# A planned two-layer long-convolution and MLP kernel: reserved engines for the first chunk, a shorter first normalisation, two half blocks that may alternate, and plain fp32 inverse transforms

## The chip, the cores and the metric

The kernel runs on one core of a Trainium2 chip. The metric is the device time of one execution in microseconds, the median of several runs. The profile shown is of one further execution, recorded by the hardware profiler.

## The reference, cut to what matters

The input is a sequence of 2048 positions with 640 channels. Two kinds of layer alternate, each twice, each with a normalisation ahead of it and a residual sum behind it:

```python
def _A_ref(q, k, v, shift_k, ssm_k, ssm_D):
    # k_shift: causal depthwise conv of k with 4 taps
    kv = k_shift * v
    # y: causal depthwise conv of kv with a kernel as long as the sequence, by FFT
    y = y + kv * ssm_D[None, None, :]
    return q * y
def _B_ref(x, w1, w2):
    h = jnp.einsum("bsd,df->bsf", x, w1)          # 640 -> 1728
    h = jnp.maximum(h, 0)
    return jnp.einsum("bsf,fd->bsd", h, w2)       # 1728 -> 640

x = A_q
x = x + _A_ref(_layernorm(x), A_k, A_v, A_shift_k, A_ssm_k, A_ssm_D)
x = x + _B_ref(_layernorm(x), B_w1, B_w2)
x = x + _A_ref(_layernorm(x), A_k, A_v, A_shift_k, A_ssm_k, A_ssm_D)
x = x + _B_ref(_layernorm(x), B_w1, B_w2)
```

The long convolution `y` doesn't depend on `x`, so both layers of kind A use the same one. All of it is in float32.

## The kernel before

**Tiling.** The sequence is cut into 8 chunks of 256 positions, each of two halves of 128 rows, and the channels into 5 tiles of 128 (`NDT`). A convolution unit is a chunk with one or two channel tiles, or two chunks with one tile. There are 21 units; `rank(u)` is a unit's place in their list, and the first three are chunk 0, the next three chunk 1.

**The convolution.** `transform(u)` loads `kt`, `vt` and the filter `hf`, adds the term `dD` to one row of `hf`, forms the taps (`acc`, `tp`), and takes a forward transform of the signal and of the filter by matmuls with constant matrices (`pg`, `pt`, `pr`). The results `at` and `gt` are spilled to memory as `A` and `G`. `products(u)` multiplies the transforms of all earlier chunks in pairs and adds them (`Ax`, `Gx`, `pd`, `pacc`, all on VectorE), forms `u`, and takes the inverse transform by matmuls into `pq`; `qs`, `ys` and `Y` are its results. Two forms of the inverse transform are there. A unit with `rank(u) < FU` is transformed in plain fp32: `cM` times `u`, which the trace shows as two records a matmul. A unit of a higher rank has `u` split in two parts of fewer bits, `uh` on ScalarE and `ul` on VectorE, and three matmuls (`mm3`) for each of the plain one's. `FU` is 10, so 11 of the 21 units take the split form, with two such groups each.

**The MLP.** The weights are loaded as fp32 (`ws`, 28 tiles of 128x640), their norm is taken by matmuls (`pw`, `pn`), and from it a scale. Each is then split in two fp16 parts (`wsplit`): the high part `w[:, 0]` on ScalarE, the low part `w[:, 1]` on VectorE. Activations are split in the same way (`xh` after the normalisation, `hh` and `hl` after the first matmul), and each product takes three matmuls. `main(n, ...)` is one MLP block. The first eight (n = 0 to 7: chunk 0 and 1, both layers, both halves apart) have 128 rows, the other twelve 256. A block goes through 7 pieces of the hidden dimension in the order `JS`: `mm1` fills `h` from the transposed input `xT`, ScalarE and VectorE make `hh` and `hl`, and `mm2` adds into `o` and `oc`. Block n starts with its first matmul into `h`.

**Chunk 0 and the head.** Nothing of the MLP can start before chunk 0's convolution is done for the first half. Its result is multiplied by the normalised input (`xnA`) and added to `x`, with the row sums in `sp`; then come the second normalisation (`sums`, `negmB`, the square `jkB`, `stdB`, the reciprocal and a Newton step on VectorE: `newton` with `fast`, then `xnB`), the split `xh`, two groups of five transposes on TensorE, and their copies to `xT`.

**What sets the order.** Every operation is given to `Plan` with an engine, an estimated cost and a priority class (`URGENT` 0, `SOON` 1, `BACK` 1.7, `SPILL`, `CONV`, `LATER`, `FILL`). `Plan.order` runs through an estimated time and, whenever an engine is free, takes from the candidates that are ready the one of the best class; the instructions are then written out in that order, and each engine runs its own in order. Buffers are rings (`Ring`): a ring's tiles are taken in the order of the program, within a `stream`; tiles of different streams may overtake each other.

Of the kernel before, what the change touches and what calls it, by code (L numbers as in the profile page):

```python
# [11 lines left out]
F32 = mybir.dt.float32  # L12
# [31 lines left out]
MODE = 0  # L44
POOLMOD = 5
STT = ((0, 0), (0, 2), (0, 4))
FA = 6
FU = 10
# [29 lines left out]
class Op:  # L78
    __slots__ = ("eng", "cost", "fn", "prio", "seq", "deps", "outs", "new", "tiles", "left", "ready", "start", "nbytes")


class Plan:
# [5 lines left out]
    def op(self, eng, cost, fn, reads=(), writes=(), prio=0, nbytes=0):  # L88
        o = Op()
        o.eng, o.cost, o.fn, o.seq, o.nbytes = eng, cost, fn, len(self.ops), nbytes  # L90
        o.prio = (prio, o.seq)
        deps, o.new, o.outs = set(), [], []
        for t in reads:
            if t.writer is not None:
                deps.add(t.writer)
        for t in writes:
            if t.writer is not None:
                deps.add(t.writer)
            elif t.ring is not None and not t.left:
# [10 lines left out]
        o.left, o.ready = len(deps), 0.0  # L110
        for d in deps:
            d.outs.append(o)
        self.ops.append(o)

    def order(self):
        engs = sorted({o.eng for o in self.ops})
        free = dict.fromkeys(engs, 0.0)
        cand = {e: [] for e in engs}
        for o in self.ops:
            if not o.left:  # L120
                cand[o.eng].append(o)
# [3 lines left out]
        while n < len(self.ops):  # L125
# [18 lines left out]
            for e in engs:  # L144
# [20 lines left out]
                if best.nbytes:  # L165
                    dma = max(dma, now + 1.9) + best.nbytes / 360e3
                    end = dma + 1.1
                if e == "PE":
# [22 lines left out]
def tile_h3_mlp(ctx: ExitStack, tc: tile.TileContext, q, kT, vT, shk, hF, hR, dD, w1, w2, cM, cG, out):  # L191
# [117 lines left out]
    def transform(u):  # L309
# [33 lines left out]
        for i, (c, t) in enumerate(u):  # L343
            if c == 0:
                dve(P, lambda i=i, t=t: DVE.tensor_add(hf[0:1, i, 0:P], hf[0:1, i, 0:P], dDs[:, t, :]), [dDs, hf], [hf], pr_)
# [32 lines left out]
        if c0:  # L378
            for b in range(2):

                def f(b=b):
                    for ri in range(2):
                        for eo in range(2):
                            m = cXt[:, ri, :] if b and eo else cGt[:, 2 * eo + ri, :]
                            PE.matmul(e4(pg[b])[:, :, ri, :], m, hv(hf)[:, eo], start=ri + eo == 0, stop=ri + eo == 2)  # L385

                pe(16 * mm4, f, [hf, cGt, cXt], [pg[b]], pr_)
                act(w, lambda b=b: ACT.activation(gt[:, :, 0:2, b, :], e4(pg[b]), AF.Copy), [pg[b]], [gt], pr_)
# [78 lines left out]
    def products(u, at, gt, after):  # L467
        n, nm = len(u), "%d_%d" % u[0]
        pr_ = (URGENT, CONV, LATER)[min(u[0][0], 2)]
        w, h = 2 * n * P, n * P  # L470
        mm, mm4 = (0.109, 0.109) if n == 2 else (0.213, 0.0545)
# [42 lines left out]
        pq = T(ps, "tr", 2, [P, 512], "pq" + nm, stream=1)  # L514
        for ri in range(2):
# [30 lines left out]
        qs = T(cv, "qs", 1, [P, n, P], "qs" + nm)  # L546
        act(h, lambda: ACT.activation(qs.t, pq[:, 256 : 256 + h].rearrange("p (a b) -> p a b", a=n), AF.Copy), [pq], [qs], pr_)
        direct = u[-1][0] == 0
        if direct:
# [5 lines left out]
            yo = lambda s: dst[s][:, t0 * P : t0 * P + h].rearrange("p (a b) -> p a b", a=n)  # L555
        else:
            ys = T(cv, "u", 2, [P, 2, n, P], "ys" + nm)
            dst = [ys, ys]
            yo = lambda s: ys[:, s]
        pp = lambda: pq[:, 0:h].rearrange("p (a b) -> p a b", a=n)  # L560
        dve(h, lambda: DVE.tensor_sub(yo(0), pp(), qs.t), [pq, qs], [dst[0]], pr_)
        dve(h, lambda: DVE.tensor_add(yo(1), pp(), qs.t), [pq, qs], [dst[1]], pr_)
# [10 lines left out]
        if direct:  # L573
            xs, xns, sp0 = first[c]
            cs = slice(t0 * P, t0 * P + h)
            for s in range(2):
                dve(h, lambda s=s: DVE.tensor_mul(xns[s][:, cs], xns[s][:, cs], dst[s][:, cs]), [xns[s], dst[s]], [xns[s]], (URGENT, BACK)[s])
                dve(h, lambda s=s: DVE.scalar_tensor_tensor(xs[s][:, cs], xns[s][:, cs], 1.0, xs[s][:, cs], op0=ALU.mult, op1=ALU.add, accum_out=sp0[s][:, 0, t0 // 2 : t0 // 2 + 1]), [xns[s], xs[s]], [xs[s], sp0[s]], (URGENT, BACK)[s], 0.2)
# [52 lines left out]
    def wsplit(k):  # L631
        for j in JS:
            for i in range(2):
# [3 lines left out]
                s = lambda: sc[k].t.bitcast(F32)  # L637
# [16 lines left out]
    def stats(xs, sums, name, S, pr=0, fast=False):  # L654
# [8 lines left out]
        if fast:  # L663

            def newton():
                stt = DVE.scalar_tensor_tensor
                r_, v_ = r[:, q_], v[:, q_]
                DVE.reciprocal(r_, sd[:, q_])
                stt(v_, ssq[:, q_], D * EPS, r_, op0=ALU.add, op1=ALU.mult)
                stt(v_, v_, -0.5 / D, r_, op0=ALU.mult, op1=ALU.mult)  # L670
                stt(r_, v_, 1.5, r_, op0=ALU.add, op1=ALU.mult)
                DVE.tensor_mul(nmr[:, q_], negm[:, q_], r_)

            dve(0, newton, [sd, ssq, negm], [r, v, nmr], pr, 0.9)
        else:
            dve(0, lambda: DVE.reciprocal(sd[:, q_], sd[:, q_]), [sd], [sd], pr, 0.15)

            def newton():
                ACT.activation(v[:, q_], ssq[:, q_], AF.Identity, scale=-0.5 / D, bias=heps.t)
                cols = [slice(s, s + 1) for s in S]  # L680
                for c in cols:
                    ACT.activation(r[:, c], v[:, c], AF.Identity, scale=sd[:, c])
                for c in cols:
                    ACT.activation(v[:, c], r[:, c], AF.Identity, scale=sd[:, c], bias=c15.t)
                for c in cols:
                    ACT.activation(r[:, c], v[:, c], AF.Identity, scale=sd[:, c])
                for c in cols:
                    ACT.activation(nmr[:, c], r[:, c], AF.Identity, scale=negm[:, c])

            act(0, newton, [ssq, sd, negm, heps, c15], [v, r, nmr], pr, 0.15 + 0.8 * len(S))  # L690
# [18 lines left out]
    SUMS = {}  # L709

    def prep(a, layer, S, pr=0):
# [20 lines left out]
        xns = stats(xs, sums2, "B" + nm, S, pr, head)  # L732
        hl = {}
        for s in S:
# [10 lines left out]
        if not head or S[0]:  # L745
            for x in range(2):
                for s in S:
                    dma(1280, lambda s=s, x=x: SP.dma_start(xt[x][:, :, (s - S[0]) * P : (s - S[0]) * P + P], hl[s][:, x, :], transpose=True), [hl[s]], [xt[x]], pr)
            return xT, S
        for x in range(2):  # L750
            pt = T(ps, *(("x", 1), ("o0", 1))[x], [P, NDT, P], f"xt{nm}{x}", F16, stream=1)

            def f(x=x, pt=pt):
                for t in range(NDT):
                    PE.transpose(pt[:, t, :], hl[0][:, x, t * P : t * P + P], ident16.t)

            pe(0.29, f, [hl[0], ident16], [pt], pr)
# [6 lines left out]
    def main(n, a, layer, S, xTS):  # L764
# [7 lines left out]
        oc = T(ps, "oc", 1, [P, 2, P], f"oc{n}")  # L772
# [20 lines left out]
        def mm1(j, i, p):  # L793
            tail = j == NFP - 1 and i == 1
            z = slice(i * R, i * R + R)

# [12 lines left out]
        for j in JS:  # L809
            p = T(ps, "h", 2, [P, 2 * R], f"h{n}_{j}")  # L810
            hh = T(mlp, "hh", NH, [P, 2 * R], f"hh{n}_{j}", F16)
            hl = T(mlp, "hl", NH, [P, 2 * R], f"hl{n}_{j}", F16)
# [22 lines left out]
        xs = X[a]  # L835
        nm = f"{a}_{layer}_{S[0]}"
        sp = T(mlp, "sp", 2, [P, 2, 2], f"sp{nm}") if layer == 0 else None
        for s in S:
            for h in range(2):

                def f(s=s, h=h):
                    d = ds[h]
                    acc = {"accum_out": sp[:, s, h : h + 1]} if layer == 0 else {}
                    DVE.scalar_tensor_tensor(xs[s][:, d], o(s, h), inv.t, xs[s][:, d], op0=ALU.mult, op1=ALU.add, **acc)

                dve(128 if h else 512, f, [oc if h else ob[s], inv, xs[s]], [xs[s]] + ([sp] if layer == 0 else []), URGENT, 0.15)
# [41 lines left out]
    def early(a):  # L888
        sums = load_x(a)
        first[a] = (X[a], stats(X[a], sums, f"A{a}_0", both, URGENT, True), [keep(const, [P, 1, 3], f"sp{a}_{s}") for s in range(2)])  # L890
# [10 lines left out]
    if MODE == 1:  # L901
        xTs.append(prep(0, 0, (1,), BACK))
# [102 lines left out]
```

## Time and profile before

| | |
|---|---|
| median of 3 runs | 875.25 us (875.15 to 875.81) |
| profiled execution | 875.43 us |
| its span in the trace | 873.7 us |
| TensorE busy | 852.4 us, 98% |
| VectorE busy | 707.5 us, 81% |
| ScalarE busy | 434.3 us, 50% |
| GpSimd busy | 1.8 us |

In the trace PE is TensorE's matmuls, PEld its weight loads, DVE VectorE, ACT ScalarE, POOL GpSimd, SP the queue that issues the DMAs; L801 is line 801 of the kernel. A row of a timeline has the start in us, the duration in us, engine, line, operation, what it writes and reads, the shape, the count, and in brackets the idle time of the engine before it with what ended it. Matmuls overlap: their rate is read from start to start, not from their durations.

### The profile page before, as it was taken

How to read it: one execution, taken by the hardware profiler on the slowest of the kernel's cores; microseconds unless marked ns; L12 is line 12 of the kernel's file. 1: busy time of each engine (PE TensorE's matmuls, PEld its weight loads, DVE VectorE, ACT ScalarE, POOL GpSimd, SP SyncE). 2: the span in 40 equal slices, each digit the busy share in tenths (PEclk: the TensorE clock that was granted, in tenths of full speed). 3: DMA queues.
4: the chain of work that ended last, by engine and by line, in shares of the span. 5: the costliest groups of instructions: out<-in, count | busy, mean ns of one | idle time of the engine just before them, and what ended most of it. 6: DMA issues, size and time to landing. Idle time of an engine off the chain costs nothing.

```text
span 873.7 us, 19067 instructions
## 1 busy us (share of the span) xinstructions
PE 852.4 (98%) x7676; PEld 652.6 (75%) x7676; DVE 707.5 (81%) x1262; ACT 434.3 (50%) x1031; POOL 1.8 (0%) x14
## 2 busy tenths in 40 slices
PE   8689999999999999999999999999999999999997
PEld 7678787787777777777777777777777777777775
DVE  7999999999989999999999999999888833323111
ACT  6497587446466364636446281825325245425010
POOL 0000000000000000000000000000000000000000
PEclk9989999999999999999999999999999999999999
DMA  9966858987997664853655947383888821201000
GB/s 324 395 240 209 275 176 287 271 298 255 302 277 221 219 208 155 248 176 133 163 192 172 235 128 199 106 247 103 254 275 258 251 73 32 61 2 31 32 1 31
DMA packets 122219, 164.12 MB, mean 188 GB/s; under 512 B 49681, under 2 KB 78609, under 8 KB 122130
## 3 DMA queue, kind: packets, MB, share of 16 engines
q1 hardware_dynamic: 122130, 162.90, 60.1%
q8 instruction: 60, 0.98, 0.5%
q14 instruction: 29, 0.24, 0.1%
HBM read 117.05 MB, written 35.65 MB: 175 GB/s over the span
## 4 chain that ended last, share of the span: by engine, by line
PE 70%; DVE 14%; DMA 8%; ACT 4%; issue 2%; SPq 1%; DVEq 0%; ACTq 0%
PE h L801 10%; PE h L802 10%; PE h L804 10%; PE o L786 8%; PE o L787 8%; PE o L789 7%; DMA Gx<-G 4%; DVE pd L510 3%; PE oc L786 2%; PE oc L787 2%; DVE pacc L511 2%; PE oc L789 2%; PE pq L531 2%; PE pg L407 2%; PE pg L385 1%
## 5 line engine op out<-in xcount | busy, mean ns | idle before, releaser
L801 PE MATMUL h<-xT,w 128*128 128x256 f16 (+1 forms) x1400 | 322.9, 252 | 0.5 <-ACT xT L761 0.5
L802 PE MATMUL h<-xT,w 128*128 128x256 f16 (+1 forms) x1400 | 322.6, 252 | 0.5 <-DMA xT<-xh 0.5
L804 PE MATMUL h<-xT,w 128*128 128x256 f16 (+1 forms) x1300 | 303.8, 252 | 0.0
L786 PE MATMUL o<-w,hh 128*128 128x512 f16 x448 | 170.0, 380 | 0.0
L787 PE MATMUL o<-w,hh 128*128 128x512 f16 x448 | 169.8, 379 | 0.0
L816 ACT ACTIVATE hh<-h 128x512 f16<-128x512 f32 (+1 forms) x120 | 60.6, 505 | 211.4 <-PE h L804 210.9
L789 PE MATMUL o<-w,hl 128*128 128x512 f16 x416 | 157.8, 379 | 1.9 <-DVE hl L817 1.9
L802 PEld LDWEIGHTS <-w 128*128 128x128 f16 x1400 | 137.4, 98 | 10.6 <-issue 0.6
L801 PEld LDWEIGHTS <-w 128*128 128x128 f16 x1400 | 137.3, 98 | 10.1 <-DMA xT<-xh 0.2
L804 PEld LDWEIGHTS <-w 128*128 128x128 f16 x1300 | 127.5, 98 | 9.7 <-issue 0.9
L817 DVE SCALAR_TENSOR_TENSOR hl<-h,hh 128x512 f16<-128x512 f32 (+1 forms) x120 | 69.4, 579 | 79.2 <-ACT hh L816 78.1
L511 DVE TENSOR_TENSOR pacc<-pacc,pd 128x768 f32<-128x768 f32 x140 | 132.9, 950 | 0.7
L787 PEld LDWEIGHTS <-hh 128*128 128x128 f16 x896 | 87.7, 98 | 56.2
L786 PEld LDWEIGHTS <-hh 128*128 128x128 f16 x896 | 87.6, 98 | 55.1 <-issue 0.7
L789 PEld LDWEIGHTS <-hl 128*128 128x128 f16 x832 | 81.4, 98 | 52.4 <-DVE hl L817 3.2
L787 PE MATMUL oc<-w,hh 128*128 128x128 f16 x448 | 98.2, 219 | 0.0
L786 PE MATMUL oc<-w,hh 128*128 128x128 f16 x448 | 98.1, 219 | 0.0
L789 PE MATMUL oc<-w,hl 128*128 128x128 f16 x416 | 91.1, 219 | 0.0
L510 DVE TENSOR_TENSOR pd<-Ax,Gx 128x768 f32<-128x768 f32 x87 | 81.5, 950 | 7.0 <-DMA Gx<-G 6.9
L339 ACT ACTIVATE tp<-kt,shs 128x256 f32<-128x256 f32 (+1 forms) x78 | 43.7, 574 | 13.8 <-DVE acc L368 6.2
L510 DVE TENSOR_TENSOR pd<-at,Gx 128x768 f32<-128x768 f32 x44 | 41.3, 949 | 0.1
L660 ACT ACTIVATE jkA<-x,negmA 128x640 f32<-128x640 f32 x32 | 26.3, 822 | 20.9 <-DVE negmA L657 20.7
(159 smaller groups left out, 1171.1 us busy)
## 6 DMA issues: line engine op xcount, KB each, us to landing
Ax<-A SPq DMA_DIRECT2D x91, 384.0 KB, 4.0
Gx<-G SPq DMA_DIRECT2D x91, 384.0 KB, 4.2
G<-gt SPq DMA_DIRECT2D x32, 384.0 KB, 3.4
A<-at SPq DMA_DIRECT2D x32, 384.0 KB, 4.3
y<-Y SPq DMA_DIRECT2D x30, 320.0 KB, 3.5
ws<-in_w SPq DMA_DIRECT2D x28, 320.0 KB, 6.7
x<-in_q SPq DMA_DIRECT2D x16, 320.0 KB, 3.9
out_dram<-x SPq DMA_DIRECT2D x16, 320.0 KB, 3.0
```

Source lines behind the costliest of these rows:

```text
L339: ACT.activation(o[:, i : i + m], kview(i, m, j), AF.Copy, scale=shs[:, t, j : j + 1])
L510: ew(f"mac{j % POOLMOD}", 768, lambda e, pd=pd, av=av, gv=gv: e.tensor_mul(pd.t, av(), gv()), [ax, gx], [pd], pr_)
L511: dve(768, lambda i=i, pd=pd: DVE.tensor_add(acc[:, i], acc[:, i], pd.t), [acc, pd], [acc], pr_)
L660: act(D, lambda s=s, jk=jk: ACT.activation(jk.t, xs[s].t, AF.Square, bias=negm[:, s : s + 1], accum_out=ssq[:, s : s + 1]), [xs[s], negm], ...
L786: PE.matmul(z, hh[:, c], wh[:, d], start=(j == JS[0] and i == 0 and (h == 0 or s == S[0])), stop=False)
L787: PE.matmul(z, hh[:, c], wl[:, d], start=False, stop=end and tail)
L789: PE.matmul(z, hl[:, c], wh[:, d], start=False, stop=end)
L801: PE.matmul(p[:, z], wh, xv(t, 0), start=b, stop=False)
L802: PE.matmul(p[:, z], wh, xv(t, 1), start=False, stop=tail and e)
L804: PE.matmul(p[:, z], wl, xv(t, 0), start=False, stop=e)
L816: act(2 * R, lambda p=p, hh=hh: ACT.activation(hh.t, p.t, AF.Relu), [p], [hh], URGENT)
L817: dve(2 * R, lambda p=p, hh=hh, hl=hl: DVE.scalar_tensor_tensor(hl.t, p.t, 0.0, hh.t, op0=ALU.max, op1=ALU.subtract), [p, hh], [hl], URGENT)
```

## The change

It has four parts.

1. **Reserved engines.** A new class `CRIT` of -1 is given to chunk 0's `transform` and `products` and to the first half's `prep`. While an operation of that class is about to become ready on an engine (all that it depends on has started), the planner doesn't start one of a lower class there whose estimated cost is more than the remaining time plus `SLACK`. The addition of `dD` to `hf` goes from VectorE (5 operations) to GpSimd (3 operations). The second half's `yd` goes to class `BACK`. `wsplit` is called once, behind the first half's `prep`, and splits the pieces of the two weights alternately, the second two pieces (`WLAG`) behind the first. The estimated costs of matmuls (`mm`, `mm4`) are raised.
2. **A shorter first normalisation.** For chunk 0's first layer, `prep` writes no normalised `xnB`. VectorE subtracts the mean (`xc`) beside ScalarE's square; `xh` and the low part `xl` come from `xc` times the reciprocal of the root. The Newton step is left to a factor for each row (`FAC`) that is applied when the block's result is added to `x`. The normalisation `xnA` of chunk 0 loses its Newton step on VectorE (`fast`) and has the ScalarE one of the other chunks.
3. **The first two half blocks may alternate.** Block 1 has streams of its own for `h`, `hh`, `hl` and `oc`. Block 0's first piece is issued as two operations, high part of `xT` first.
4. **Inverse transforms.** `FU` is 99: all 21 units are transformed back in plain fp32.

```diff
-MODE = 0
+WLAG = 2
+CRIT, SLACK = -1, 0.6
-FU = 10
+FU = 99
@@ Plan.order
+        soon = {e: [o for o in self.ops if o.eng == e and o.prio[0] == CRIT] for e in engs if e != "SP"}
...
+                rooms = [(max(d.ready for d in o.deps) - now + SLACK, o.prio) for o in soon.get(e, ()) if o.left and all(d.start is not None for d in o.deps)]
                 for o in cand[e]:
                     if best is not None and o.prio > best.prio:
+                        continue
+                    if any(o.cost > room and o.prio > prio for room, prio in rooms):
                         continue
@@ transform, products
-        pr_ = (URGENT, CONV, LATER)[min(u[0][0], 2)]
+        pr_ = (CRIT, CONV, LATER)[min(u[0][0], 2)]
-        mm, mm4 = (0.109, 0.109) if n == 2 else (0.213, 0.0545)
+        mm, mm4 = (0.128, 0.113) if n == 2 else (0.213, 0.063)
-        for i, (c, t) in enumerate(u):
-            if c == 0:
-                dve(P, lambda i=i, t=t: DVE.tensor_add(hf[0:1, i, 0:P], hf[0:1, i, 0:P], dDs[:, t, :]), [dDs, hf], [hf], pr_)
+        if c0:
+            t0 = u[0][1]
+            gps(h, lambda: POOL.tensor_add(hf[0:1, :, 0:P], hf[0:1, :, 0:P], dDs[:, t0 : t0 + n, :]), [dDs, hf], [hf], pr_)
@@ wsplit
-    def wsplit(k):
-        for j in JS:
+    def wsplit():
+        ks = [(JS[x - y * WLAG], y) for x in range(NFP + WLAG) for y in range(2) if 0 <= x - y * WLAG < NFP]
+        for j, k in ks:
@@ prep, chunk 0's first layer
+            dve(D, lambda: DVE.tensor_scalar(xc.t, xs[s].t, negm[:, 0:1], None, op0=ALU.add), [xs[s], negm], [xc], pr)
+            act(1, lambda: ACT.activation(sd[:, 0:1], ssq[:, 0:1], AF.Sqrt, scale=1.0 / D, bias=epst.t), [ssq, epst], [sd], pr, 0.1)
+            dve(1, lambda: DVE.reciprocal(r[:, 0:1], sd[:, 0:1]), [sd], [r], pr, 0.15)
+            act(D, lambda: ACT.activation(w.t, xc.t, AF.Copy, scale=r[:, 0:1]), [xc, r], [w], pr)
+            dve(D, lambda: DVE.scalar_tensor_tensor(v.t, xc.t, r[:, 0:1], w.t, op0=ALU.mult, op1=ALU.subtract), [xc, r, w], [v], pr, 0.13)
...
+            dve(0, factor, [ssq, r, inv], [fac, FAC[a, s]], CONV, 0.6)
@@ main
-        oc = T(ps, "oc", 1, [P, 2, P], f"oc{n}")
+        sm = 3 if n == 1 else 0
+        oc = T(ps, *(("x", 1) if n == 1 else ("oc", 1)), [P, 2, P], f"oc{n}", stream=sm)
...
-            p = T(ps, "h", 2, [P, 2 * R], f"h{n}_{j}")
+            p = T(ps, "h", 2, [P, 2 * R], f"h{n}_{j}", stream=sm)
@@ the order of the program
-    wsplit(0)
-    xTs = [prep(0, 0, (0,))]
-    if MODE == 0:
-        xTs.append(prep(0, 0, (1,), BACK))
-    wsplit(1)
+    xTs = [prep(0, 0, (0,), CRIT)]
+    xTs.append(prep(0, 0, (1,), BACK))
+    wsplit()
```

More of the change, by code (lines that the diff above doesn't have):

```diff
@@ L78 @@
 class Op:
-    __slots__ = ("eng", "cost", "fn", "prio", "seq", "deps", "outs", "new", "tiles", "left", "ready", "start", "nbytes")
+    __slots__ = ("eng", "cost", "fn", "prio", "seq", "deps", "outs", "new", "tiles", "left", "ready", "start", "nbytes", "deps")
 class Plan:
@@ L109, in op @@
         deps.discard(o)
-        o.left, o.ready = len(deps), 0.0
+        o.left, o.ready, o.start, o.deps = len(deps), 0.0, None, deps
         for d in deps:
@@ L167, in order @@
                     end = dma + 1.1
+                best.ready = end
+                if best.prio[0] == CRIT and e in soon:
+                    soon[e].remove(best)
                 if e == "PE":
@@ L379, in transform, with f @@
             for b in range(2):
-                def f(b=b):
-                    for ri in range(2):
+                for ri in range(2):
+                    def f(b=b, ri=ri):
                         for eo in range(2):
@@ L652, in small, with stats @@
         return T(mlp, tag, 2, [P, 2], name)
-    def stats(xs, sums, name, S, pr=0, fast=False):
+    def stats(xs, sums, name, S, pr=0):
         q_ = slice(S[0], S[-1] + 1)
@@ L661, in stats, with newton @@
         act(2, lambda: ACT.activation(sd[:, q_], ssq[:, q_], AF.Sqrt, scale=1.0 / D, bias=epst.t), [ssq, epst], [sd], pr, 0.1)
[L663 to L690, printed above, removed]
+        dve(0, lambda: DVE.reciprocal(sd[:, q_], sd[:, q_]), [sd], [sd], pr, 0.15)
+        def newton():
+            ACT.activation(v[:, q_], ssq[:, q_], AF.Identity, scale=-0.5 / D, bias=heps.t)
+            cols = [slice(s, s + 1) for s in S]
+            for c in cols:
+                ACT.activation(r[:, c], v[:, c], AF.Identity, scale=sd[:, c])
+            for c in cols:
+                ACT.activation(v[:, c], r[:, c], AF.Identity, scale=sd[:, c], bias=c15.t)
+            for c in cols:
+                ACT.activation(r[:, c], v[:, c], AF.Identity, scale=sd[:, c])
+            for c in cols:
+                ACT.activation(nmr[:, c], r[:, c], AF.Identity, scale=negm[:, c])
+        act(0, newton, [ssq, sd, negm, heps, c15], [v, r, nmr], pr, 0.15 + 0.8 * len(S))
         xns = {}
@@ L795, in mm1, with f @@
             z = slice(i * R, i * R + R)
+            if n == 0 and j == JS[0]:
+                def f(x):
+                    for t in range(NDT):
+                        b, e = t == 0, t == NDT - 1
+                        wh, wl = w1at(j, t, i, 0), w1at(j, t, i, 1)
+                        PE.matmul(p[:, z], wh, xv(t, x), start=b and x == 0, stop=e and x == 1)
+                        if not x:
+                            PE.matmul(p[:, z], wl, xv(t, 0), start=False, stop=False)
+                for x in range(2):
+                    pe((10 - 5 * x) * 0.0545 * len(S), lambda x=x: f(x), [xT[0, x], WT[j, 0, 0], WT[j, 0, 1]], [p], FILL)
+                return
             def f():
@@ L835, in main @@
         xs = X[a]
+        fac = {s: FAC.get((a, s), inv) if layer == 0 else inv for s in S}
         nm = f"{a}_{layer}_{S[0]}"
@@ L889, in early @@
         sums = load_x(a)
-        first[a] = (X[a], stats(X[a], sums, f"A{a}_0", both, URGENT, True), [keep(const, [P, 1, 3], f"sp{a}_{s}") for s in range(2)])
+        first[a] = (X[a], stats(X[a], sums, f"A{a}_0", both, URGENT), [keep(const, [P, 1, 3], f"sp{a}_{s}") for s in range(2)])
     early(0)
```

65 lines of the change are left out of this document (40 added, 25 removed).

## The prediction

> **What bounds the kernel now.** I read the page first, then windows cut at the events of the head, then the timeline of the head, the waits, and the groups by shape.
>
> ```profile
> PE 852.4 (98%) x7676; PEld 652.6 (75%) x7676; DVE 707.5 (81%) x1262; ACT 434.3 (50%) x1031; POOL 1.8 (0%) x14
> ```
>
> ```profile
> 33.00:40.40 7.40, 4.16 (x49) 3.38 (x49) 7.40 (x26) 4.53 (x7) 0.00 (x0) 1.00 1.06 388
> 40.40:48.00 7.60, 2.01 (x13) 1.50 (x14) 7.35 (x20) 7.60 (x15) 0.00 (x0) 0.50 1.07 400
> 48.00:50.64 2.64, 2.64 (x26) 2.64 (x26) 2.48 (x7) 2.02 (x4) 0.00 (x0) 0.50 0.86 278
> ...
> 180.00:310.00 130.00, 127.10 (x1339) 99.88 (x1339) 123.96 (x223) 73.25 (x180) 0.00 (x0) 1.00 0.81 254
> 310.00:700.00 390.00, 389.11 (x3187) 291.94 (x3186) 371.98 (x590) 186.70 (x441) 0.00 (x0) 1.00 0.65 195
> ```
>
> The columns are the window, its length, the busy time of PE, PEld, DVE, ACT and POOL, the granted clock and the DMA's share and rate. PE has no room from 48 us on: it idles 2.9 us in 180 to 310 and 0.9 in 310 to 700. Its one large hole is the head: from 33 to 48 us it works 6.2 of 15, while DVE has none free. So two things can move the time: when PE gets steady work, and how much work it has behind that.
>
> ```profile
> 35.97 0.88 DVE L639 SCALAR_TENSOR_TENSOR w<-ws,wsc,w 128x640 f16<-128x640 f32 x1
> ...
> 38.27 0.46 PE L610 MATMUL pw<-ws 128*128 128x128 bf16 x5 [0.35 <-DMA ws<-in_w]
> ...
> 39.16 0.15 DVE L719 TENSOR_REDUCE sums<-sp 128x1 f32<-128x3 f32 x1
> ...
> 40.88 0.81 ACT L660 ACTIVATE jkB<-x,negmB 128x640 f32<-128x640 f32 x1
> ...
> 42.14 0.16 DVE L668 RECIPROCAL rstdB<-stdB 128x1 f32<-128x1 f32 x1
> ...
> 42.92 0.16 DVE L672 TENSOR_TENSOR nmrB<-negmB,rstdB 128x1 f32<-128x1 f32 x1
> ...
> 44.98 0.72 ACT L736 ACTIVATE xh<-xnB 128x640 f16<-128x640 f32 x1
> ...
> 45.76 0.72 PE L755 MATMUL xt<-ident,xh 128*128 128x128 f16 x5 [4.80 <-ACT xh L736]
> 45.91 0.82 DVE L737 TENSOR_TENSOR xh<-xnB,xh 128x640 f16<-128x640 f32 x1
> ...
> 47.25 0.68 ACT L761 ACTIVATE xT<-xt 128x640 f16<-128x640 f16 x1
> ...
> 47.98 0.27 PE L801 MATMUL h<-xT,w 128*128 128x128 f16 x1 [0.48 <-ACT xT L761]
> ```
>
> This is the chain that opens PE's work: the row sums at 39.16, the square, the reciprocal at 42.14, the split, the transposes, the first MLP matmul at 47.98. Weight splits (L639) stand between its steps. Ten of the 28 pieces are split by 48 us, so PE never waits for weights later.
>
> **The head: the chain.** The raised costs and the reservations change only the order, so I read the order that the changed kernel is built with. One piece's low part is split there ahead of the first half's `xl`, and none ahead of the sums.
>
> ```profile
> L345 DVE TENSOR_TENSOR hf<-hf,dDs 1x128 f32<-1x128 f32 x5 | 1.4, 273 | 1.0 <-DMA dDs<-in_dD 1.0
> ```
>
> ```profile
> 54.34 1.68 DVE L639 SCALAR_TENSOR_TENSOR w<-ws,wsc,w 128x640 f16<-128x640 f32 x2
> ```
>
> Two splits in 1.68 us, one lasting 0.88, make 0.80 from start to start. Three stood ahead of the sums: 2.4 us gone. The five additions to `hf` leave DVE: 1.4 busy, some 1.0 as they follow each other. The Newton step of `xnA` leaves it too: five starts from 42.14 to 42.92 are 0.2 each, four go, 0.8. Against that DVE now waits for `acc`, for `qs` and for `xnA`, since ScalarE does nine small Newton operations; I set 0.8 for it, an estimate, about a third of what those operations take.
>
> ```profile
> L682 ACT ACTIVATE rstdA<-varA,stdA 128x1 f32<-128x1 f32 x30 | 7.4, 288 | 3.5 <-DVE stdA L676 3.1
> ```
>
> At 0.29 each they are under 2.6 us of ScalarE, which is 4.5 of 7.4 us busy there. So the sums come at 39.2 - 2.4 - 1.0 - 0.8 + 0.8 = 35.8, the square at 36.2, the reciprocal 1.26 later (40.88 to 42.14) at 37.5. `xh` is now one operation of 0.72, since the mean was taken off beside the square: 38.3. Transposes 0.72 and the copy 0.68, behind one split on ScalarE, give `xT` at 39.8. On DVE: one split to 38.4, `xl` (0.8) to 39.2, the copy of the low part to 40.5, the second split to 41.4. The second transposes stand behind the norm of the last weight, which lands at 38.27 as before, so this can't come much earlier. PE has six matmuls from 40.1 and the rest of the first block from 41.4, against 47.98. The three operations of `factor` for each half cost 0.2 each, as in the Newton step that they replace, and come when nothing of the chain waits; behind them only the block's sum does, some 30 us later.
>
> The additions on GpSimd are not in the trace. The nearest row is a cast:
>
> ```profile
> 1.64 0.29 POOL L247 CAST ident<-ident 128x128 f16<-128x128 f32 x1
> ```
>
> ```profile
> 3.19 3.90 DMA dDs<-in_dD
> 8.11 3.72 PE pg L385 x16
> ```
>
> (From the chain that ended last: start, time, what.) I take 0.5 for the first addition, an estimate between this row and 1.5, five times as much. `dDs` lands at 7.1, and PE began `pg` at 8.11, behind two additions on DVE; so it is a gain of 0.4 to a loss of 0.6, and the work of DVE between `pg` and the sums, which isn't moved by it, hides at least half of either. The Trainium skill (SBUF — State Buffer, "SBUF: two separate sides") says that a GpSimd operation and a DVE operation with two SBUF inputs exclude each other for their whole length; no run here shows it yet, and it would add at most one such operation to each.
>
> **The head: starved of weights.** What DVE doesn't split ahead of 41.4, it splits while PE wants it. Between that and the split that feeds the fourth piece's `mm2` stand 18 splits, two 640-wide operations (`xc`, `xl`), four `hl`, four 512-wide additions and some small ones.
>
> ```profile
> L353 DVE TENSOR_TENSOR gs<-hf,hr 128x512 f32<-128x512 f32 x34 | 23.0, 682 | 0.0
> ...
> L817 DVE SCALAR_TENSOR_TENSOR hl<-h,hh 128x256 f16<-128x256 f32 x48 | 20.0, 416 | 1.3 <-ACT hh L816 1.0
> ```
>
> Each less the 0.08 that neighbours overlap, and `xc` and `xl` as the low part at 45.91: 18 x 0.80 + 2 x 0.74 + 4 x 0.34 + 4 x 0.60 + 0.7 = 20.3, to about 61.7 us. What PE has in its built order up to there goes at these rates:
>
> ```profile
> 82.26 0.38 PE L789 MATMUL o<-w,hl 128*128 128x512 f16 x1
> 82.47 0.22 PE L786 MATMUL oc<-w,hh 128*128 128x128 f16 x1
> 82.53 0.22 PE L787 MATMUL oc<-w,hh 128*128 128x128 f16 x1
> ...
> 82.64 0.22 PE L801 MATMUL h<-xT,w 128*128 128x128 f16 x1
> ```
>
> 0.216 for 512 columns and 0.056 for 128. The rest of the first piece's `mm1` is 1.3, three more at 30 x 0.056 are 5.0, four `mm2` at 6 x (0.216 + 0.056) are 6.5, block 1's first `mm1` 1.7, most of the sixth piece's 1.4, and eight filter-transform records 1.7: 17.6. The first of them begins at 41.4 and the last `mm2` can't end before 62.4, 0.8 behind its weights: 21.0 us, of which PE waits 3.2 to 3.4, for the third and fourth pieces' weights above all. What follows has its weights. On SP the first 56 issues stand as before; the second half's transposes now stand among the loads of chunk 1's products, and must land by 54 us, some 5 behind their `xl`, or block 1 delays what is queued behind it on PE.
>
> At 82.64, in the last row, block 1's third piece begins, and the set of matmuls ahead of it is the same in both orders. PE was busy all the 34.7 us from 47.98 to there, of which 1.3 are lost to the half clock from 48 to 50.64: 33.3. The changed kernel gets there at 41.4 - 0.3 + 33.3 + 3.2 = 77.6, or, if the clock stays at half until 50.6, at 78.7, since PE then catches up in its waits. **Gain 3.9 to 5.0; I take 4.4.** The clock was 0.50 from 40.4 on, behind 38 to 40 us with hardly a matmul. The Trainium skill (TensorE: Matmul & The Clock Gate, "What's actually happening") says that a window of about 3.4 us without activity halves the clock and a busy one restores it; by that rule, which the rows of 0.50 bear out, the thinner start may keep the half clock longer, which is the 1.1.
>
> **Plain inverse transforms.** 22 groups change their form. One of each, and the next matmul behind it:
>
> ```profile
> 181.63 1.08 PE L531 MATMUL pq<-u,cM 128*128 128x256 f32 x4
> 182.55 0.38 PE L786 MATMUL o<-w,hh 128*128 128x512 f16 x1
> ```
>
> ```profile
> 451.30 0.22 PE L789 MATMUL oc<-w,hl 128*128 128x128 f16 x1
> 451.33 0.37 PE L276 MATMUL pq<-uh,cMh 128*128 128x256 f32 x1
> ...
> 452.13 0.28 PE L801 MATMUL h<-xT,w 128*128 128x256 f16 x1
> ```
>
> Plain: 0.92. Split: 0.80, begun 0.03 early (0.03 behind the matmul before it, where 0.06 is usual), so 0.77. 22 x 0.15 = **+3.3**. But not all split groups ran so:
>
> ```profile
> 303.56 0.37 PE L276 MATMUL pq<-uh,cMh 128*128 128x256 f32 x1
> ...
> 304.97 0.28 PE L801 MATMUL h<-xT,w 128*128 128x256 f16 x1
> ```
>
> ```profile
> L538 DVE TENSOR_TENSOR ul<-u,uh x22: 676/682/693, 272.6 to 701.3; 128x512 fp32r<-128x512 f32 x22
> ```
>
> This one took 1.41, 0.6 too long, waiting for `ul`. The waits name three such:
>
> ```profile
> PEld pq L277 <- DVE ul L538: 1.2, 3, 0.5
> ```
>
> In plain form this wait is gone; PE may wait for `u` itself, but that comes a ScalarE and a DVE operation earlier. I take back 1.0 of the 1.2. DVE loses 22 x 0.68 = 15.0 us (the row's middle number is its median in ns, then come the first and last start). Most lies in 310 to 700, where PE idles 0.9 us; there it is worth nothing.
>
> **Sum.** The profiled execution took 875.43, its span and 1.73 around it, 0.18 over the median. 875.43 - 4.4 + 3.3 - 1.0 = 873.3; less 0.18, **873.1**. A difference of 0.2% (1.75 us: under 873.5 or over 877.0) is about what a measurement can tell.
>
> **Rivals.**
>
> *The gain is eaten by DVE before 310 us; slower.* In 180 to 310 DVE is 124 of 130 us busy, and PE waits for it:
>
> ```profile
> PE o L789 <- DVE hl L817: 1.9, 2, 1.2
> ```
>
> ```profile
> 286.38 0.27 PE L801 MATMUL h<-xT,w 128*128 128x256 f16 x1
> ```
>
> If DVE sets when the first full block (n = 8) can begin, here, PE only waits more, and the plain form is paid behind it: 875.25 + 3.3, less a third of the 1.2, the one wait for `ul` that I find behind 310 us: 878.1. It decides if that block begins later than about 285. Against it: in the built order DVE has some 4 us less ahead of the last pieces of block 6 (fewer small operations, and PE's blocks set earlier beside it), so it should be early too. 20%.
>
> *Half the head's gain.* GpSimd slow, ScalarE late with high parts, the second half's `xT` late: each wait shifts all that follows, as splits queue behind. Gain 2.2 instead of 4.4: 875.3, no change to be told. 22%.
>
> *DVE's relief is worth more.* The 2.9 us that PE idles in 180 to 310 mostly go, with DVE ahead of plan: another 2.5, 870.6. For it: the waits named are for DVE. Against it: the first `ul` starts at 272.6, so little of that stretch is relieved. 18%.
>
> **How the numbers follow.** The forecast has 40%; its own range, 872.0 to 874.5, is the clock's 1.1 and the 1.2 of waits. Eight in ten needs the others' centres, **870.0 to 878.0**: half of the slower rival and half of the fastest, 19%, lie outside. Faster: all of the third rival and some 0.29 of the forecast, 0.47; slower: the first rival and 0.01, 0.21; same 0.32.
>
> **What would show it.** Right: first block's matmuls at 40 to 42 us, PE idle some 3 us from 42 to 62, block 1's third piece at 77.6 to 78.7, groups of `pq` at 0.92 everywhere, DVE 14 us less busy. Wrong: block 1's third piece behind 80.5 us (the head), or at 78 with n = 8 beginning at 285 or later (the first rival), or PE idle over 4 us behind 310.

## The result, and the profile after

| | before | after |
|---|---|---|
| median, 15 runs each | 874.24 us (871.61 to 875.81) | 878.59 us (876.01 to 882.51) |
| ratio to before | | 1.0052 (95%: 1.0036 to 1.0068) |
| profiled execution | 875.43 us | 878.59 us |
| its span | 873.7 us | 876.8 us |

The change made the kernel slower by 4.4 us (3.1 to 5.9 by the interval), where 2.2 us faster was forecast. After's 15 times fall into two groups: nine lie at 876.0 to 879.2 us (median 877.25), six, the upper group, at 880.4 to 882.5 (median 881.4); the profiled execution is one of the nine. The first line of the page, and the windows at the cuts of before (PE, PEld, DVE, ACT, POOL, granted clock, DMA):

```profile
PE 858.6 (98%) x7632; PEld 652.7 (74%) x7632; DVE 694.1 (79%) x1231; ACT 424.9 (48%) x1016; POOL 4.1 (0%) x17
```

```profile
33.00:40.40 7.40, 4.66 (x53) 3.78 (x51) 6.43 (x29) 5.13 (x10) 0.00 (x0) 0.91 1.05 379
40.40:48.00 7.60, 7.32 (x85) 6.92 (x83) 6.29 (x16) 6.49 (x15) 0.00 (x0) 0.64 1.02 401
48.00:50.64 2.64, 2.45 (x28) 1.57 (x26) 2.42 (x5) 2.64 (x5) 0.00 (x0) 1.00 0.14 57
180.00:310.00 130.00, 129.47 (x1351) 101.45 (x1350) 127.00 (x228) 71.49 (x178) 0.00 (x0) 1.00 0.87 275
310.00:700.00 390.00, 388.82 (x3126) 290.01 (x3125) 361.26 (x571) 177.06 (x422) 0.00 (x0) 1.00 0.66 196
```

TensorE's hole in the head is closed (7.3 of 7.6 us busy, before 2.0), and VectorE is 13.4 us less busy. Yet the span is 3.1 us longer. The timeline of the head:

```profile
36.30 0.15 DVE L715 TENSOR_REDUCE sums<-sp 128x1 f32<-128x3 f32 x1
...
38.16 0.16 DVE L739 RECIPROCAL rstdB<-stdB 128x1 f32<-128x1 f32 x1 [0.39 <-ACT stdB L738]
...
39.31 0.71 PE L776 MATMUL xt<-ident,xh 128*128 128x128 f16 x5 [2.00 <-ACT xh L740]
...
41.39 0.27 PE L824 MATMUL h<-xT,w 128*128 128x128 f16 x1
...
43.62 0.31 PE L824 MATMUL h<-xT,w 128*128 128x128 f16 x1
43.73 0.31 PE L826 MATMUL h<-xT,w 128*128 128x128 f16 x1
...
81.05 0.22 PE L836 MATMUL h<-xT,w 128*128 128x128 f16 x1
...
285.25 0.27 PE L836 MATMUL h<-xT,w 128*128 128x256 f16 x1
```

The first MLP matmul comes 6.6 us earlier (41.39, before 47.98), block 1's third piece only 1.6 earlier (81.05, before 82.64). In the five profiles below that have after's head (after, e1, e3, e5, e9) the third piece begins at 81.05 to 82.38, in the three that have before's (before, e2, e11) at 82.64 to 83.78: 1.5 apart in the mean. The first full block, n = 8, begins at 285.25, before at 286.38. At 43.6 matmuls of 128 columns start 0.11 apart, twice the usual 0.056: the clock is at half from 39.1 to 45.9.

For a ledger I take the time from one mark to the next, less TensorE's work between them in the order as built, each matmul at its undisturbed rate from start to start (0.056, 0.109 and 0.216 us for 128, 256 and 512 columns, 0.92 for a plain group of `pq`). What is left is lost to waits and to the half clock. The ledger is of the two profiled executions, which are 3.2 us apart and not 4.4, since the one of before is 1.2 over its median:

| us | before | after | difference | forecast |
|---|---|---|---|---|
| first MLP matmul at | 47.98 | 41.39 | -6.6 | -6.6 |
| lost from there to block 1's third piece | 1.1 | 6.1 | +5.0 | +2.2 |
| lost from there to n = 8 | 4.8 | 5.9 | +1.1 | 0 |
| lost behind n = 8 | 1.7 | 2.1 | +0.4 | -1.0 |
| work of the plain inverse transforms | | | +3.25 | +3.3 |
| sum | | | +3.1 | -2.1 |

### The profile page after: what moved, and what is told of

Same layout as the page of the kernel before. It is cut to its first block, busy times and chain, and to the rows that moved or that the text cites. A ratio compares the mean times of both kernels' runs of the same rounds, so it can differ in the third digit from the quotient of the medians.

```text
span 876.8 us, 18920 instructions
## 1 busy us (share of the span) xinstructions
PE 858.6 (98%) x7632; PEld 652.7 (74%) x7632; DVE 694.1 (79%) x1231; ACT 424.9 (48%) x1016; POOL 4.1 (0%) x17
## 4 chain that ended last, share of the span: by engine, by line
PE 79%; DVE 9%; DMA 6%; ACT 3%; issue 2%; SPq 1%; DVEq 0%; ACTq 0%
PE h L836 11%; PE h L837 11%; PE h L839 11%; PE o L808 9%; PE o L809 9%; PE o L811 8%; PE pq L540 4%; PE oc L809 2%; PE oc L808 2%; PE oc L811 2%; PE pg L415 2%; DVE pd L518 1%; DMA y<-Y 1%; DMA Gx<-G 1%; DVE pacc L519 1%
## 5 line engine op out<-in xcount | busy, mean ns | idle before, releaser
L540 PE MATMUL pq<-u,cM 128*128 128x256 f32 (+1 forms) x168 | 43.5, 384 | 2.6 <-DVE u L534 2.4
```

The source lines that it names most:

```text
L540: PE.matmul(pq[:, ri * 256 : ri * 256 + h], cMt[:, ri + 4 * kk, :], fv()[:, :, kk, :], start=kk == 0, stop=kk == 1)
```

## The experiments

Each time is a median against the kernel before on the same chip (874.1 to 874.9 there). The executions of one kernel begin the MLP up to 1 us apart, so marks of single profiles are compared to that. Theory: the plain form is paid in full, and the head's gain is lost to waits for split weights and to the half clock. Rivals: the loss sits in the order before n = 8, in VectorE's load, or in single waits.

**e1, the split form back, and e2, the plain form alone.**

```diff
 e1, in the changed kernel        e2, in the kernel before
-FU = 99                         -FU = 10
+FU = 10                         +FU = 99
```

> The changed kernel with FU = 10 again: 11 units take the split inverse transform, all else as changed. Theory (the plain form costs TensorE 0.15 us for each of 22 groups and is paid in full, since TensorE has no room behind 300 us): 878.6 - 3.3 = 875.3, up to 1.0 more where the waits for the low part of u come back. Rival (the time is lost in the order of the first 300 us, and the plain form is hidden or repaid by VectorE's relief): 878 to 879, as before this edit.

> The kernel before with FU = 99 and nothing else of the change. Theory: 874.2 + 3.3, less 0 to 1.0 for the waits for the low part of u that go: 876.5 to 877.5. Rival (VectorE's 15 us of relief repay it): 874 or below.

e1: 873.73 us, ratio 0.9995 (0.9977 to 1.0012). e2: 879.42 us, ratio 1.0053 (1.0041 to 1.0066). So the plain form alone makes the slowdown, and all the rest of the change is worth at most 2 us, with zero inside the interval. By the medians the price is 4.5 (e2; 3.6 to 5.8 by its interval) to 4.9 (878.59 - 873.73), above the 3.3 of its work. The 4.9 holds a second thing: six of after's 15 runs are in the upper group, and only one of e1's 12 (881.29; the others end at 876.2). Without these the medians are 877.25 and 873.72, 3.5 apart. In e2's timeline TensorE waits for `u` at the head of a plain group:

```profile
533.97 1.13 PE L531 MATMUL pq<-u,cM 128*128 128x256 f32 x4 [1.39 <-DVE u L522]
534.94 0.27 PE L801 MATMUL h<-xT,w 128*128 128x256 f16 x1
```

**e11, more work without another form.**

```diff
+                PE.matmul(o, cMs[0][:, ri, :], uh[:, :, 0, :], start=True, stop=True)
                 for kk in range(2):
```

> The kernel before with one more matmul of 256 columns in each of the 22 split groups, a repeated product that the next one overwrites: 22 x 0.13 = 2.9 us of TensorE, no other operation, no other wait. Theory (the plain form costs its 3.3 us of TensorE, and the rest of the 4.7 measured comes from waits for u that stand in place of those for ul): 874.5 + 2.9 = 877.4. Rival (TensorE's work costs more than itself, as it pushes other work late): 878.5 to 879.

876.46 us, ratio 1.0023 (1.0013 to 1.0033): 2.2 us more, where the groups' median went from 0.796 to 0.911 us, 22 x 0.115 = 2.5. TensorE's work costs itself, not more.

**e12, the plain form a third time** (FU = 99 in the kernel of e10, below).

> The kernel of e10 with FU = 99: plain inverse transforms for all units, the 34 transposes of the identity, and ys in the ring of uh and ul, which no unit then uses otherwise. It measures the plain form a third time, without the waits at 112 us. Theory (3.3 us of work, and 1.0 to 1.5 of waits for u in place of those for ul): 871.3 + 4.5 = 875.8. Rival (the plain form costs its work alone, and what the two other pairs showed above it was chance): 871.3 + 3.3 = 874.6.

875.77 us, ratio 1.0026 (1.0016 to 1.0036): 4.4 above e10, with no upper group in either. So in two pairs the form costs 1.1 and 1.2 more than its work, and in the third (after and e1) 0.2 to 1.6, as the upper group is left out or counted. Behind 286 us, TensorE's gaps ahead of `pq` for `u` add up to 0.2 to 2.2 us in the seven profiles with plain transforms (mean 1.2), those for `ul` to 0 to 1.4 in the nine with the split form (mean 0.4). The means differ by some 0.8; where the rest lies stays open.

**e3, a buffer of its own for `ys`.** After's timeline, SP's rows first, then VectorE's and TensorE's:

```profile
104.53 1.12 SPq L579 DMA_DIRECT2D Y<-ys x2
```

```profile
DMA to landing us min/median/max: 3.3/3.6/6.7
```

```profile
108.40 0.67 DVE L531 TENSOR_TENSOR u<-pacc 128x512 f32<-128x512 f32 x1
111.81 0.69 DVE L533 TENSOR_TENSOR u<-pacc 128x512 f32<-128x512 f32 x1 [2.73 <-DMA A<-at]
```

```profile
114.41 1.13 PE L540 MATMUL pq<-u,cM 128*128 128x256 f32 x4 [2.08 <-DVE u L534]
```

`u` and `ys` share a ring of two buffers. The second `u` needs the slot of a `ys` whose store was issued at 105.0 and took 6.7 us to land (the second row's largest), behind a burst of other transfers. The row names `A<-at`; that one landed only at 114. VectorE stands for 2.7 us, TensorE for 2.1.

```diff
-            ys = T(cv, "u", 2, [P, 2, n, P], "ys" + nm)
+            ys = T(cv, "ys", 1, [P, 2, n, P], "ys" + nm)
-    cMs = csplit(cMt, 6)
+    cMs = csplit(cMt, 4)
```

> The changed kernel with a buffer of its own for the results ys, which otherwise lie in the ring of u and hold it until their store has landed (the room comes from splitting four instead of six of the constant matrices, the other two being unused with plain inverse transforms). Theory (VectorE waits 2.7 us at 109 us, and TensorE 2.1 at 112, for a landing store of ys, not for work): both waits go, 878.6 - 2.1 = 876.5; if the upper level of times (880 to 882.5) comes from that wait together with the clock, all runs lie at 874 to 877. Rival (VectorE has no free time before 300 us, so what is won at 112 is lost again by the first full block): n = 8 begins at 285 as before the edit, 878.6.

879.15 us, ratio 1.0046 (1.0034 to 1.0058). The wait is gone, but n = 8 begins at 286.07 with 0.9 us more work done ahead of it: the order behind 120 us is another, and has 1.9 us of other waits. The rival's outcome. The five runs lie at 877.8 to 879.9: none is in the upper group, but none is under the median of after's lower one either.

That group goes with the clock. In after its six runs have mean granted clocks of 0.991 to 0.994, the nine others 0.995 to 0.998, and one more window of 3.41 us at half clock takes 0.002 off the mean of 877 us. e1's profiled execution was its one run above 877 (881.29). Its windows, cut where the clock changes:

```profile
112.79:116.20 3.41, 1.25 (x18) 1.06 (x16) 2.99 (x6) 0.87 (x3) 0.00 (x0) 1.00 0.45 151
116.20:119.62 3.42, 3.42 (x21) 2.60 (x20) 2.38 (x5) 2.09 (x5) 0.00 (x0) 0.50 0.61 211
```

The wait at 113 fell into one window of 3.41 us whole, and the next ran at half clock. In after's profiled execution the same gap lies in a window that is busy 1.58 us, and the clock stays:

```profile
110.75:114.16 3.41, 1.58 (x21) 1.17 (x19) 2.35 (x5) 0.29 (x1) 0.00 (x0) 1.00 0.48 191
```

The clock isn't the whole of it. One window at half clock takes at most 1.7 us of TensorE's work (half of 3.41), while after's two groups are 4.1 apart and e1's 881.29 is 7.6 over its median. Where the rest goes isn't shown.

**e4, filler in the head.**

```diff
+            for _ in range(NWARM if s == 0 else 0):
+                pe(0.057, lambda: PE.matmul(fill[:, 0:P], ident16.t, ident16.t, start=True, stop=True), [ident16, negm], [fill], IDLE)
```

> The changed kernel with 40 matmuls of the identity (128 columns) added while the first half's mean is taken off and split, so that TensorE isn't idle from 37.3 to 39.3 us; the result isn't used. Theory A (the half clock from 39.2 to 46.0 us costs TensorE 2.1 us): the clock stays at 1.00, block 1's third piece begins at 79 instead of 81.05, 876.5. Theory B (TensorE is starved of split weights from 47 to 72 us, so it waits longer for the same weights): the clock stays at 1.00, but block 1's third piece begins at 80.5 to 81, 878.3.

878.64 us (874.88 to 883.81), ratio 1.0044 (1.0024 to 1.0063), no gain, though the clock stayed at 1.00 in the profiled execution. The planner gave the head another order, in which block 1's third piece came earlier than either theory had it:

```profile
76.43 0.22 PE L839 MATMUL h<-xT,w 128*128 128x128 f16 x1
...
282.54 0.27 PE L839 MATMUL h<-xT,w 128*128 128x256 f16 x1
```

Against after that is 4.6 us at the third piece, 2.7 at n = 8, 2.0 at the end of this profile, and nothing in the median. Part of the 4.6 was never won. Between the first MLP matmul and the third piece this order has 8 records of a filter transform, after's 16 (e4, then after):

```profile
L416 PE MATMUL pg<-gs,cG 128*128 128x256 f32 x8 | 2.2, 399 | 0.6 <-DVE gs L362 0.6
```

```profile
L415 PE MATMUL pg<-gs,cG 128*128 128x256 f32 x16 | 4.1, 390 | 0.0
```

At 0.216 us each, 1.7 us of the 4.6 is work put off, and it is done by n = 8. The other 2.9 is nearly all still there at n = 8 (2.7). Behind that the median shows none of it, but with runs this far apart e4 doesn't decide whether it lasts.

**e5, VectorE relieved, and e9, relieved and with the buffer of e3.**

```diff
+            add = lambda i=i, pd=pd: DVE.tensor_add(acc[:, i], acc[:, i], pd.t)
+            dve(768, add if u[-1][0] > 3 else lambda: None, [acc, pd], [acc], pr_)
```

> The changed kernel, in the same planned order, with the 30 additions into pacc of the chunks 1 to 3 left out (part of the convolution isn't computed): 30 x 0.87 = 26 us less for VectorE between 81 and 285 us, nothing less for TensorE. Theory (VectorE, 96% busy there, sets when n = 8 can begin, so TensorE waits 5.9 us on the way): the waits fall under 2.5 us, n = 8 begins at about 281.5, 875. Rival (the waits come from landing DMAs and from where single groups stand in TensorE's order, not from VectorE's load): n = 8 begins at 285 and the time stays at 878 to 879.

> The changed kernel with both: 30 additions into pacc of the chunks 1 to 3 left out (part of the convolution isn't computed), and a buffer of its own for ys. Theory (two limits in series before n = 8, VectorE's load and the wait for a landing store, of which each takes the other's place): TensorE's waits from 81 to 285 us fall from 5.9 to under 2.5, n = 8 begins at 281 to 282, 874.5. Rival (VectorE's relief alone had given all there is): 876.7, n = 8 at 284.

e5: 876.72 us, ratio 1.0033 (1.0018 to 1.0047). e9: 877.54 us, ratio 1.0039 (1.0024 to 1.0054). The same window of after and of e5:

```profile
82.00:285.00 203.00, 199.88 (x2189) 158.22 (x2187) 192.87 (x367) 122.70 (x309) 0.00 (x0) 1.00 0.83 258
```

```profile
82.00:285.00 203.00, 201.53 (x2217) 160.04 (x2216) 172.03 (x341) 122.61 (x309) 0.00 (x0) 1.00 0.83 262
```

VectorE has 20.8 us less to do, and in these two profiles TensorE loses 2.1 us less on the way (3.8, not 5.9). The median falls by 1.9, but the intervals of the two ratios overlap (after's begins at 1.0036), so a gain at the end of the kernel isn't shown. In e5's profile n = 8 begins 0.9 earlier, at 284.36, and at 674 us more than that is lost again. The longest wait behind n = 8, after and then e5:

```profile
PE h L862 <- DVE hl L857: 1.1, 1, 1.1
```

```profile
PE h L863 <- DVE hl L858: 2.8, 1, 2.8
```

So VectorE's load is a part of what TensorE loses before n = 8, but both theories fail in e9: with both limits gone, 4.0 us are still lost, most of it in many small waits (`gs`, `sl` and `at` of single units, 0.3 to 0.7 each).

**e6, filler in an unchanged order, and e8, filler in the kernel before.**

```diff
+                for _ in range(NWARM if S == (0,) and not x else 0):
+                    PE.transpose(pt[:, 0, :], ident16.t, ident16.t)
                 for t in range(NDT):
```

> The changed kernel with FU = 10 and 34 transposes of the identity ahead of the first half's transposes, in an otherwise unchanged order, so that TensorE works from 37.3 to 39.2 us; their result is overwritten. Theory A (the half clock costs TensorE some 2 us behind 41 us, and they last to the end): 873.7 - 2 = 871.7. Theory B (what the head wins is taken back by waits for VectorE before n = 8): block 1's third piece 2 us earlier, n = 8 less than 0.7 earlier, 873.3.

> The kernel before with 26 matmuls ahead of the second norm's sum and 76 transposes of the identity ahead of the first half's transposes, so that TensorE is busy from 38.7 to 45.7 us; their results are overwritten. Theory A (the half clock from 40.4 to 50.6 us costs 1.3 us, and they last): the clock stays at 1.00, 874.9 - 1.3 = 873.6. Theory B (waits for VectorE before n = 8 take it back): 874.9.

e6: 872.87 us, 0.9 under e1, ratio 0.9989 (0.9977 to 1.0002). e8: 873.44 us, ratio 0.9989 (0.9979 to 0.9999). After's and e6's windows:

```profile
39.20:46.00 6.80, 6.42 (x58) 6.03 (x59) 5.22 (x14) 5.76 (x13) 0.00 (x0) 0.51 1.05 401
```

```profile
39.20:46.00 6.80, 5.33 (x85) 4.82 (x86) 6.32 (x16) 6.80 (x16) 0.00 (x0) 1.00 1.04 401
```

At full clock TensorE does 85 matmuls instead of 58, and waits instead: from the first matmul to the third piece it loses 5.6 us, where e1 loses 6.9 and after 6.1. So 0.5 to 1.3 us of what the half clock takes is still missing at the third piece; the rest would have been waited anyway. In e8 the filler leaves one window at half clock, which ends at 45.95, before the first MLP matmul (48.68 in its profile), and TensorE loses nothing from there to the third piece (before: 1.1). So the half clock is worth about 1 us in both kernels, at the edge of what the intervals separate from nothing.

**e7, no alternation.**

```diff
-        sm = 3 if n == 1 else 0
+        sm = 0
-        oc = T(ps, *(("x", 1) if n == 1 else ("oc", 1)), [P, 2, P], f"oc{n}", stream=sm)
+        oc = T(ps, "oc", 1, [P, 2, P], f"oc{n}", stream=sm)
```

> The changed kernel with FU = 10 and without streams of its own for block 1, so the first two half blocks can't alternate. Theory (while the split weights are scarce, block 1's pieces use a weight a second time, and save TensorE 2 us or more of waiting between 41 and 72 us): 873.7 + 1 to 2 = 875 to 876. Rival (the pieces only change places, and VectorE's time before n = 8 decides): 873.7.

874.63 us, ratio 1.0006 (0.9993 to 1.0020), and block 1's third piece at 82.43 (e1: 82.38). What alternation is worth, 0.9 by the medians, isn't separated from nothing; at the third piece it is nothing.

**e10, split form, filler, and `ys` in another ring.**

```diff
-            ys = T(cv, "u", 2, [P, 2, n, P], "ys" + nm)
+            ys = T(cv, *(("u", 2) if rank(u) >= FU else ("ru", NRU)), [P, 2, n, P], "ys" + nm)
```

> The changed kernel with FU = 10, the 34 transposes of the identity ahead of the first half's transposes, and ys of the units below rank 10 in the ring of uh and ul, which they don't use. Theory (without the slot's wait at 112 us, and with VectorE a little less late than in the plain form): 872.9 - 2 = 871. Rival (VectorE's load before n = 8 takes it back, as with plain inverse transforms): 872.9.

871.34 us (871.02 to 873.72), ratio 0.9969 (0.9957 to 0.9982): faster than both kernels, by 3 us (1.6 to 3.8) and by 7. Against e6 the median falls by 1.5, of a removed wait of 2 us. So here it seems to last, though the two intervals just overlap (e6's begins at 0.9977) and the order behind the head isn't quite e6's.

**e13, VectorE relieved in the head, and e14, no reservation** (both in the kernel of e10).

```diff
 e13
+            ew(f"tap{j}", w, add if u[0] != (1, 0) else lambda e: None, [acc, tp], [acc], pr_)
+        ew("kv", w, kv if u[0] != (1, 0) else lambda e: None, [acc, vt], [acc], pr_)
 e14
-                    if any(o.cost > room and o.prio > prio for room, prio in rooms):
+                    if False:
```

> The kernel of e10, in the same planned order, with four 512-wide operations of VectorE left out of the transform of chunk 1's first unit (three additions of taps and the product with vt, between 59 and 68 us; part of the convolution isn't computed): 4 x 0.6 = 2.4 us less for VectorE before 72 us, nothing less for TensorE. Theory (from 41 to 72 us VectorE's low parts of the weights and hl set when TensorE goes on): of the 5.7 us that TensorE waits there 1.2 go, those at 62 to 71 us, block 1's third piece is that much earlier, 870.2. Rival (ScalarE's high parts set it, or later waits take it back): 871.3.

> The kernel of e10 with the first chunk's class kept, but without the reservation: the planner may start other work on an engine that the first chunk needs next. Theory (what is split before 41 us needn't be split while TensorE waits for it; an earlier first matmul is mostly paid back by block 1's third piece): the first MLP matmul 1 to 2 us later, the third piece within 0.7, 871.3 to 872. Rival (an earlier start lasts): third piece and time later by as much as the first matmul, 872.5 to 873.3.

e13: 871.71 us, ratio 0.9975 (0.9959 to 0.9990): no gain. The waits at 63 to 72 us fell from 1.2 to 0.7, and in this profile one window at half clock outweighs that. e14: 874.84 us, ratio 1.0002 (0.9989 to 1.0014). The first MLP matmul and block 1's third piece, e10 and then e14:

```profile
41.34 0.22 PE L827 MATMUL h<-xT,w 128*128 128x128 f16 x1
...
80.55 0.22 PE L839 MATMUL h<-xT,w 128*128 128x128 f16 x1
```

```profile
45.53 0.22 PE L827 MATMUL h<-xT,w 128*128 128x128 f16 x1 [0.39 <-ACT xT L785]
...
79.93 0.22 PE L839 MATMUL h<-xT,w 128*128 128x128 f16 x1
```

Beginning 4.2 us later costs the third piece nothing: TensorE loses 0.9 us on the way instead of 5.7. In e14 seven of the 28 low parts are split ahead of the first matmul, in e10 one, and the last ends at 70.6 us, not 73.0. So e10's earlier start is bought with splits that TensorE then waits for; e14's is followed by work almost without a wait. The time is 3.5 us longer all the same, by the medians (1.4 between the two profiled executions). Its order differs behind the head too, and which of its waits make that up is open.

## Why the prediction was wrong

Two steps failed: that the head wins 4.4 us and keeps them to the end, and that the plain form gives back 1.0 of the 3.3 that its work costs.

**Right.** The first MLP matmul at 41.39, where six were forecast from 40.1 and the rest of the piece from 41.4, behind sums at 36.3 and the reciprocal at 38.2, each 0.5 to 0.7 late; 14 us of VectorE (13.4); the plain groups at 0.92 us (median 0.919 behind 270 us); their work of 3.3 (3.25).

**Head: mis-sized, 4.4 forecast and 1.6 seen.** The step "starved of weights" counted 3.2 us of waits, and at most 1.1 more for the clock; 6.1 were lost. The half clock halved TensorE's rate for the 4.1 us that it worked from 41.4 to 45.9, which is 2.0, but part of that it makes up in its waits: e6, with the clock at 1.00, still loses 5.6. So the mis-sized term is the waits, 5.6 where the sum has 3.2; the clock's 0.5 (after) to 1.3 (e1) is about what the range allows for it. The fourth piece had its last weights at 63.8, not 61.7, and its `mm2` ended at 64.4, not 62.4. Of these 2.1 us 1.1 are there at once, as the second split ended at 42.5 and not at 41.4, and 0.8 are VectorE's own wait for the first piece's `hh`, which the sum didn't have:

```profile
41.65 0.88 DVE L648 SCALAR_TENSOR_TENSOR w<-ws,wsc,w 128x640 f16<-128x640 f32 x1
...
45.67 0.42 DVE L852 SCALAR_TENSOR_TENSOR hl<-h,hh 128x256 f16<-128x256 f32 x1 [0.84 <-ACT hh L851]
```

Behind it, where "what follows has its weights", TensorE waited once more for parts of `h` that stand in VectorE's queue among the splits:

```profile
PE h L836 <- DVE hl L852: 0.7, 1, 0.7
PE h L836 <- DVE hh L864: 0.2, 1, 0.2
```

By the prediction's own mark (third piece behind 80.5) the head was wrong. e14 beside e10 shows the deeper error: TensorE's earlier start of 6.6 us was charged with 2.2 of losses, while the splits that it postpones come back as waits almost in full.

**Gains that last: wrong.** The sum carried the head's gain to the end. By e1 all of the change but the plain form is worth 0.4 us by its ratio, at most 2.0. The first rival, a gain eaten before n = 8, had 20% and gave 878.1; n = 8 begins at 285.25, behind its mark of 285, and 878.59 was measured. Its mechanism was right in part: relieving VectorE saves TensorE 2.1 us before n = 8 (e5), but the largest single wait (2.1 at 112) is for a buffer slot whose store lands late, at a place that the trace of before doesn't show as a wait. That its end is so near is in part luck: it starts from 875.25 where 15 runs gave 874.24, and adds 2.9 for the plain form.

**Plain form: +3.3 - 1.0 forecast, +4.4 to 4.9 measured by the medians.** The work was right. The 1.0 taken back for waits on `ul` has the wrong sign: 1.1 and 1.2 came on top in two of the three pairs and 0.2 to 1.6 in the third, in part as waits for `u` itself (1.39 us in one place of e2). The upper group of times wasn't in the sum at all: without it after's median is 877.25, with it 878.59. No run shows a gain from VectorE's relief behind 310 us, as the prediction had it.

## What to carry to other kernels

Before pricing an earlier start, find what ends last in the stretch behind it: if another engine's queue has to be worked off anyway, the first engine only waits elsewhere. Where every engine runs in a fixed order and two are about 95% busy or more, a wait removed in one place can return at the next (e3, e9), so test a gain at the end of the kernel and not at its place. When two marks are compared across orders, count the work ahead of each: an order that puts work off looks early (e4). Work on the bound engine, in contrast, is paid in full (e11): a form that costs it 0.15 us a group must give the time back on that same engine.

## What the runs showed of the hardware

Clock changes lie on a grid of 3.41 us, and the grid's place differs between executions, so that the same gap costs nothing or a window at half clock. The Trainium skill (TensorE: Matmul & The Clock Gate, "What's actually happening") says that the window is free-running; the traces agree. An idle window isn't needed: one that was busy 1.25 of 3.41 us halved the clock, one with 1.58 didn't, but in e13 one with 1.95 did (the window behind it ran at 0.50), so the busy share of a trace doesn't tell it:

```profile
38.86:42.27 3.41, 1.95 (x28) 1.43 (x25) 2.90 (x7) 3.38 (x8) 0.00 (x0) 1.00 1.07 390
```

GpSimd's addition to `hf` takes 0.7 to 0.8 us in after's trace (estimated at 0.5) and holds up VectorE:

```profile
9.69 0.76 POOL L353 TENSOR_TENSOR hf<-hf,dDs 1x256 f32<-1x256 f32 x1 [2.36 <-DMA hf<-in_hF]
9.80 0.94 DVE L380 TENSOR_TENSOR sd<-acc 128x256 f32<-128x256 f32 x1
...
13.43 0.42 DVE L380 TENSOR_TENSOR sd<-acc 128x256 f32<-128x256 f32 x1
```

The same operation takes 0.42 alone and 0.94 beside it, as the Trainium skill has it (SBUF — State Buffer, "SBUF: two separate sides"); in the prediction no run showed it yet. It is 0.5 us for an addition over one partition.
